# The first attention unit's scores and softmax in two halves, with its loads as first part, mask, second part

## The chip, the cores and the metric

One core of one Trainium2 chip runs the kernel. The metric is device microseconds (us) of one execution; lower is better.

## The reference

The kernel computes three stages one after the other: a local attention with a few global tokens, and two feed-forward layers.

```python
# attention: B, H, Sl, D = 4, 8, 512, 64, 32 global tokens, window 32
out_g = np.matmul(sm(s_g), v_all)                    # global queries see all keys
mask = np.abs(pos[:, None] - pos[None, :]) <= window # local queries see the window
s_l = np.concatenate([s_lg, np.where(mask, s_ll, -1e9)], axis=-1)
out_l = np.matmul(sm(s_l), np.concatenate([v_g, v_l], axis=2))
# first layer, d_ff = 1536
x = (silu(x @ w_gate) * (x @ w_val)) @ w_out
# second layer, d_ff = 2048
h = x @ w_in
out = (np.maximum(h, 0) + alpha * np.minimum(h, 0)) @ w_out
```

## The kernel before, in words

The attention works in units. A local unit (class Local) is one batch and one pair of heads: 16 blocks of 32 queries (NB is 16), each against a stretch of 128 gathered keys. `mm` makes the scores of the unit into two PSUM banks, one per head; `soft(h)` does the softmax of one head in four pieces of 128 rows by 128 keys: on DVE an addition of the mask `lm` with a row minimum (the scores are negated), on ACT an exponential with a row sum. `t(h)` transposes the four pieces of a head on PE and copies them from PSUM to the tile `pt`; the copy goes to ACT or to DVE by `evac`, in the share that `cp0` gives while the head of the program runs. `pv` multiplies with the values on PE and scales by the reciprocal row sums on DVE into the tile `o`, of which there is one buffer. `to` transposes `o` on PE; for batch 0 ACT writes the high part of it into `xa` and DVE the low part. Each float32 feed-forward product is made of three products of such parts.

The program starts with the four local units of batch 0, here called u0 to u3. Their loads are first in SP's queue: the keys and queries `qk` of u0 in two parts, the mask, then `qk` and the values `v` of the other units and the first weights. Weights of the first layer come as 64-bit floats and are converted by ACT and DVE (`raw`, `dbl`, `y`, `yp` in the profile) into a high and a low half `w`. While they land, `heat` issues 98 small matmuls on PE. Then the first layer visits batch after batch (`g`, `v`, `acc` in the profile, line 273), with the attention of the next batch between its matmuls; from about 405 us on a part runs without recording (lines 1245 to 1456).

The order of the work until then is not that of the code. Every operation is recorded by a Planner, in atoms (the operations of one engine inside one `with nc.atom()` stay together). `order` plays the atoms through a list schedule with fixed costs, takes at each step, of those that are ready within LOOK, the one that is due first, and `flush` issues them. So every recorded instruction has line 273, and tiles have to tell them apart. A change in the first atoms can alter the order of all that is planned after them.

The prediction's steps speak of `mm` and `soft` of Local (lines 449 to 487), of `evac` with `cp0`, of `pv` and `to`, and of the list `steps` at line 1062, which gives the order in which the head is recorded.

Of the kernel before, what the change touches and what calls it, by code (L numbers as in the profile page):

```python
# [19 lines left out]
B, H, S, G, D = 4, 8, 512, 32, 64  # L20
# [7 lines left out]
NB = S // 32  # L28
NPOS = 26
WIN = 32 * NPOS  # L30
# [7 lines left out]
    lo0=0.0, lo1=0.0, lo2=0.0, lo3=0.0, hi0=0.0, hi1=0.25, hi2=0.25, hi3=0.5,  # L38
    wl0=2, wl1=2, wd=2, tsim=False,
    hq0=0.0, hq1=0.0, hq2=0.0, hq3=0.0, pr_s=0, pr_pv=0, pr_conv=0, pr_hilo=0, pr_st=0, pr_ld=0, pr_h=0,  # L40
    pr_xp=0, pr_acc=0, pr_lda=0, wage=3, w2n=2, w2max=200, cp0=0.5, cp1=0.0,
)


def pos(i):

    return 3 * (i // 2) + i % 2
# [275 lines left out]
def kernel(  # L323
# [11 lines left out]
    nc = Planner(tc)  # L335
# [49 lines left out]
    lm = attc.tile([128, 4, 128], BF16, name="lm")  # L385
# [6 lines left out]
    def att_bank():  # L392
        t = att_tags["list"][att_tags["i"] % len(att_tags["list"])]
        att_tags["i"] += 1
        return bank(t)
# [4 lines left out]
    def heat(n, cols):  # L400

        t = bank("g")
        with nc.atom():
            for _ in range(n):
                nc.tensor.matmul(
                    out=t[0:cols, 0:cols], lhsT=zero[:, 0:cols], rhs=zero[:, 0:cols], start=True, stop=True
                )
# [37 lines left out]
    class Local(Unit):  # L445
        def __init__(self, pair):
            self.pair = pair

        def mm(self):
            x = self.pair.qk  # L450
            self.s = [att_bank(), att_bank()]
            with nc.atom():
                for i in range(NB):
                    t, c = divmod(i, 4)
                    for h in (1, 0):
                        rows = slice(D * h, D * h + D)
                        nc.tensor.matmul(
                            out=self.s[h][32 * c:32 * c + 32, 128 * t:128 * t + 128],
                            lhsT=x[rows, WIN + 32 * i:WIN + 32 * i + 32],
                            rhs=x[rows, 32 * pos(i):32 * pos(i) + 128],  # L460
                            start=True,
                            stop=True,
                        )
            self.e = attp.tile([128, 2, 4, 128], F32, tag="e", name="e")
            self.sm = attp.tile([128, 16], F32, tag="sm", name="sm")[:, 0:8]
            self.mx = attp.tile([128, 16], F32, tag="mx", name="mx")

        def soft(self, h):
            with nc.atom():
                for t in range(4):  # L470
                    j = 2 * t + h
                    nc.vector.tensor_tensor_reduce(
                        out=self.e[:, h, t],
                        in0=self.s[h][:, 128 * t:128 * t + 128],
                        in1=lm[:, t],
                        scale=-0.125,
                        scalar=3e38,
                        op0=ALU.add,
                        op1=ALU.min,
                        accum_out=self.mx[:, j:j + 1],  # L480
                    )
                for t in range(4):
                    j = 2 * t + h
                    nc.scalar.activation(
                        out=self.e[:, h, t], in_=self.e[:, h, t], func=ACTF.Exp, scale=-1.0, bias=self.mx[:, j:j + 1],
                        accum_out=self.sm[:, j:j + 1],
                    )
# [219 lines left out]
    def wload(now=False):  # L707
        if wq and not wq[0][3]:
            keys, src, pool, _, age = wq[0]
            if st["w"] < age + P["wage"] and not now:  # L710
                return False
            wq.popleft()
            at = pool.next("w")
            t = wtile(pool)
            if callable(src):
                src(t, at)
                return True
            with pr("ld"):
                nc.sync.dma_start(out=t.bitcast(F32), in_=src)
            put(keys, t)  # L720
            return True
        if wq and len(wloaded) < (ND if st["k"] < mark[2] - 4 else 2):
            keys, src, pool, _, _ = wq.popleft()
            raw = dbl_tile()
            with pr("ld"):
                nc.sync.dma_start(out=raw.rearrange("p (i c) -> p i c", i=2), in_=src)
            wloaded.append([keys, raw, pool, st["w"]])
            return True
        return False
# [50 lines left out]
    def wpump():  # L780
        ready = list(wsplit)
        wsplit.clear()
        wlow()
        while wloaded and wloaded[0][3] <= st["w"] - (P["wl0"] if st["k"] < mark[4] else P["wl1"]):
            e = wloaded.popleft()
            dbl = e[1]
            e[1] = raw = raw_tile()
            convert(dbl, raw)
            wsplit.append(e)
        for keys, raw, pool, _ in ready:  # L790
            raw = raw.rearrange("p (i c) -> p i c", i=2)
            t = wtile(pool)
            z = "0" if st["k"] < mark[1] else "1" if st["k"] < mark[2] else "2"
            with pr("hilo"):
                if frac("hi" + z):
                    nc.vector.tensor_copy(t[:, :, 0], raw)
                else:
                    nc.scalar.activation(out=t[:, :, 0], in_=raw, func=ACTF.Copy)
            wlo.append((keys, raw, t, st["w"], z))
        if not P["wd"]:  # L800
            wlow()
        st["w"] += 1
# [237 lines left out]

    if True:
        p0 = pairs[0]
        p0[0].load_qk(0)
        heat(HEAT, 128)
        heat(P["TINY"], 32)
        with nc.atom():
            p0[0].load_qk(1)
            nc.sync.dma_start(out=lm, in_=lmask)
        p0[1].load_qk()
        make_identity(nc.nc, ident)  # L1050
        p0[2].load_qk()
# [1 line left out]
        for f, p in zip((0, 1, 2, 3, 0, 4, 5, 2, 4), ("gv", "gv", "gv", "gv", "o", "gv", "gv", "o", "o")):  # L1053
# [6 lines left out]
        nc.sync.dma_start(out=gm[:, :, 0], in_=gmask)  # L1060
        u0, u1, u2, u3 = head
        steps = [
            [u0.mm, (u0.soft, 0), u1.mm, (u0.soft, 1)],
            [(u0.t, 0), (u1.soft, 0), (u0.t, 1), u2.mm, (u1.soft, 1)],
            [u0.pv, (u1.t, 0), (u2.soft, 0)],
            [u0.to, (u1.t, 1), u3.mm, (u2.soft, 1)],
# [6 lines left out]
        ]  # L1073
        for i, fs in enumerate(steps):
            for f in fs:
                f[0](f[1]) if isinstance(f, tuple) else f()
            if i >= 2:
                wload()
            wpump()
# [255 lines left out]
        for j in range(NF1 // 2):  # L1335
# [10 lines left out]
            h = hring[j % 2]  # L1346
# [239 lines left out]
```

## Time and profile before

| what | us |
|---|---|
| median of 3 runs | 885.64 (882.5 to 888.14) |
| the profiled execution | 882.67 |
| its span | 880.9 |
| PE busy | 865.6 (98%) |
| ACT busy | 527.1 (60%) |
| DVE busy | 690.1 (78%) |

The span runs from the first to the last instruction; the profiled execution is 1.77 us longer, for what lies around it. PE is TensorE's matmul, PEld its weight load, DVE VectorE, ACT ScalarE, SP the queue that issues the transfers. A row of the timeline gives start, duration, engine, line, operation, tiles written and read, and in brackets the idle time of the engine before it and what ended that; "issue" is a wait for which the profile shows no releaser.

### The profile page before, as it was taken

Reading aid. Unit: us, or ns where it says so; the run is one execution under the profiler, and the core shown is the slowest. Engines: PE = TensorE matmul, PEld = TensorE weight load, DVE = VectorE, ACT = ScalarE, POOL = GpSimd, SP = SyncE. Lnnn points to the kernel's source line nnn. Section 1 sums busy time; section 2 is a strip of 40 time slices with the busy share of each in tenths; the row PEclk is TensorE's granted clock in tenths of the full one; section 3 lists DMA queues with packets and bytes.
Section 4 is the critical chain, followed back from the end, with each engine's and each line's share of the span. In section 5 each row is a group of like instructions: output and inputs, shape, how many; then the busy total and the mean of one; then the engine's idle time right before and its main releaser. Section 6 shows DMA issues by size and latency. Waiting matters only on the chain.

```text
span 880.9 us, 17473 instructions
## 1 busy us (share of the span) xinstructions
PE 865.6 (98%) x6946; PEld 750.5 (85%) x6946; DVE 690.1 (78%) x1441; ACT 527.1 (60%) x1051; POOL 0.7 (0%) x6
## 2 busy tenths in 40 slices
PE   7899999999999999999999999999999999999997
PEld 6677778888788777888999999988999988999996
DVE  4897999989877857597766697777896777967776
ACT  6899999878586877654333346343645434553442
POOL 0000000000000000000000000000000000000000
PEclk8999999999999999999999999999999999999999
DMA  9899899899969799985566576364474645585631
GB/s 350 327 399 405 346 363 379 321 366 384 414 240 353 282 334 337 371 296 183 169 246 227 186 273 239 144 244 186 193 279 178 257 168 214 218 301 214 273 144 61
DMA packets 41666, 239.31 MB, mean 272 GB/s; under 512 B 4848, under 2 KB 5488, under 8 KB 19312
## 3 DMA queue, kind: packets, MB, share of 16 engines
q1 hardware_dynamic: 41584, 238.19, 71.6%
q8 instruction: 55, 0.90, 0.4%
q14 instruction: 27, 0.22, 0.1%
HBM read 183.38 MB, written 54.79 MB: 270 GB/s over the span
## 4 chain that ended last, share of the span: by engine, by line
PE 89%; DMA 5%; ACT 2%; DVE 2%; issue 1%; SPq 0%; ACTq 0%; DVEq 0%
PE ps_acc L1456 21%; PE acc L273 11%; PE g L273 10%; PE ps_g L1245 9%; PE ps_v L1245 9%; PE v L273 9%; PE ps_a L1245 8%; PE a L273 6%; PE ps_acc L1302 3%; PE ps_a L1302 2%; DMA dbl<-in_w_dram 1%; DMA qk<-in_qk_dram 1%; DMA w2so<-dbl 1%; DMA w2sx<-dbl 1%; DMA yp<-in_w_dram 1%
## 5 line engine op out<-in xcount | busy, mean ns | idle before, releaser
L1456 PE MATMUL ps_acc<-w,hring 128*128 128x512 f32 x816 | 194.2, 391 | 0.0
L1456 PEld LDWEIGHTS ps_acc<-w,hring 128*128 128x128 f32 x816 | 152.0, 188 | 30.1 <-ACT hring L1425 0.3
L273 PE MATMUL g<-xa,w 128*128 128x512 f32 x432 | 107.7, 397 | 1.0 <-ACT sg L273 0.4
L273 PE MATMUL v<-xa,w 128*128 128x512 f32 x432 | 107.0, 396 | 0.0
L273 PE MATMUL acc<-h,w 128*128 128x512 f32 x432 | 106.1, 394 | 0.0
L1420 ACT ACTIVATE r<-c 128x384 f32<-128x384 f32 (+1 forms) x96 | 47.9, 498 | 93.2 <-DVE c L1253 93.2
L1461 DVE TENSOR_TENSOR oacc<-ps_acc,oacc 128x512 f32<-128x512 f32 x119 | 81.9, 691 | 21.9 <-PE ps_acc L1456 20.7
L273 PEld LDWEIGHTS g<-xa,w 128*128 128x128 f32 x432 | 79.0, 188 | 20.8 <-ACT sg L273 1.5
L273 PEld LDWEIGHTS acc<-h,w 128*128 128x128 f32 x432 | 79.8, 188 | 18.6 <-issue 1.8
L273 PEld LDWEIGHTS v<-xa,w 128*128 128x128 f32 x432 | 79.3, 188 | 18.4 <-issue 1.4
L1425 ACT ACTIVATE hring<-g 128x384 fp32r<-128x384 f32 (+1 forms) x96 | 48.6, 506 | 55.8 <-DVE g L1422 55.5
L1426 DVE TENSOR_TENSOR hring<-g,hring 128x384 fp32r<-128x384 f32 (+1 forms) x96 | 51.1, 532 | 18.9 <-ACT hring L1425 16.1
L1422 DVE SCALAR_TENSOR_TENSOR g<-g,nal,r 128x384 f32<-128x384 f32 (+1 forms) x96 | 56.8, 591 | 10.6 <-ACT g L1421 10.0
L273 ACT ACTIVATE e<-e,mx 128x128 f32<-128x128 f32 (+1 forms) x136 | 57.2, 423 | 10.6 <-DVE mx L273 10.3
L273 ACT ACT_TABLE_LOAD x46 | 59.0, 1283 | 5.6 <-PE g L273 4.1
L1421 ACT ACTIVATE g<-c 128x384 f32<-128x384 f32 (+1 forms) x96 | 47.9, 499 | 13.7 <-DVE hring L1426 13.7
L1245 PE MATMUL ps_g<-xa,w 128*128 128x320 f32 (+1 forms) x288 | 53.4, 319 | 0.2
L1245 PE MATMUL ps_v<-xa,w 128*128 128x320 f32 (+1 forms) x288 | 53.2, 319 | 0.1
L1245 PE MATMUL ps_a<-w 128*128 128x384 f32 (+1 forms) x288 | 51.4, 326 | 0.0
L1245 PEld LDWEIGHTS ps_g<-xa,w 128*128 128x128 f32 x288 | 47.1, 188 | 1.9 <-ACT p L1261 0.4
L1245 PEld LDWEIGHTS ps_v<-xa,w 128*128 128x128 f32 x288 | 46.9, 188 | 1.6 <-DVE u L1269 0.4
L1245 PEld LDWEIGHTS ps_a<-w 128*128 128x128 f32 x288 | 47.9, 188 | 0.1
(209 smaller groups left out, 1403.1 us busy)
## 6 DMA issues: line engine op xcount, KB each, us to landing
dbl<-in_w_dram SPq DMA_DIRECT2D x28, 1024.0 KB, 7.7
w<-w2so SPq DMA_DIRECT2D x24, 1024.0 KB, 5.3
w<-w2sx SPq DMA_DIRECT2D x24, 1024.0 KB, 4.8
w<-w2ss SPq DMA_DIRECT2D x24, 1024.0 KB, 6.8
v<-in_v_dram SPq DMA_DIRECT2D x15, 1024.0 KB, 10.8
qk<-in_qk_dram SPq DMA_DIRECT2D x14, 688.0 KB, 8.7
w2sx<-dbl SPq DMA_DIRECT2D x8, 1024.0 KB, 5.9
w2so<-dbl SPq DMA_DIRECT2D x8, 1024.0 KB, 9.2
```

The source lines that it names most:

```text
L273: last[o.eng] = getattr(getattr(self.nc, o.eng), o.op)(*o.args, **o.kw)
L1245: nc.tensor.matmul(out=o[:, 0:n], lhsT=left(name, a, k), rhs=x[name][:, b, k, 0:n], start=(i == 0), stop=(i == 5),)
L1302: mm = nc.tensor.matmul(out=o, lhsT=a, rhs=x, start=(first and e == 0 and not second), stop=((j, f, e) == (NF1 // 2 - 1, 0, 2) and i not i ...
L1420: nc.scalar.activation(out=rr, in_=u, func=ACTF.Relu)
L1421: nc.scalar.activation(out=g, in_=u, func=ACTF.Relu, scale=-1.0)
L1422: nc.vector.scalar_tensor_tensor(out=g, in0=g, scalar=nal[:, i:i + 1], in1=rr, op0=ALU.mult, op1=ALU.add)
L1425: nc.scalar.activation(out=hi, in_=g, func=ACTF.Copy)
L1426: nc.vector.tensor_tensor(out=lo, in0=g, in1=hi, op=ALU.subtract)
L1456: nc.tensor.matmul(out=o, lhsT=a, rhs=x, start=(i == 0), stop=(i == 5))
L1461: nc.vector.tensor_tensor(out=oacc[tb], in0=o, in1=oacc[tb], op=ALU.add)
```

## The change

Three things are edited. `mm` can put its score matmuls into several atoms, and `soft` can take some of the four pieces; u0 uses both with two halves. The two parts of u0's `qk` and the mask are one atom, recorded in the order first part, mask, second part, ahead of `heat`. And `cp0` goes from 0.5 to 0.75: six instead of four of the eight copies of `pt` in the head are made by DVE.

```diff
-    pr_xp=0, pr_acc=0, pr_lda=0, wage=3, w2n=2, w2max=200, cp0=0.5, cp1=0.0,
+    pr_xp=0, pr_acc=0, pr_lda=0, wage=3, w2n=2, w2max=200, cp0=0.75, cp1=0.0,
...
-        def mm(self):
+        def mm(self, halves=1):
             x = self.pair.qk
             self.s = [att_bank(), att_bank()]
-            with nc.atom():
-                for i in range(NB):
...
+            for k in range(halves):
+                with nc.atom():
+                    for i in range(NB // halves * k, NB // halves * (k + 1)):
...
-        def soft(self, h):
+        def soft(self, h, ts=range(4)):
             with nc.atom():
-                for t in range(4):
+                for t in ts:
...
         p0 = pairs[0]
-        p0[0].load_qk(0)
+        with nc.atom():
+            p0[0].load_qk(0)
+            nc.sync.dma_start(out=lm, in_=lmask)
+            p0[0].load_qk(1)
         heat(HEAT, 128)
         heat(P["TINY"], 32)
-        with nc.atom():
-            p0[0].load_qk(1)
-            nc.sync.dma_start(out=lm, in_=lmask)
...
-            [u0.mm, (u0.soft, 0), u1.mm, (u0.soft, 1)],
+            [(u0.mm, 2), (u0.soft, 1, (0, 1)), (u0.soft, 0, (0, 1)), (u0.soft, 0, (2, 3)), u1.mm, (u0.soft, 1, (2, 3))],
```

In SP's queue before, the two transfers of the second part came first, then the mask, then the two of the first part; now the first part's two are first, the mask is third as before, and the second part's two follow. No other transfer moves until the 27th. The planner's order of the rest moves with the change. On PE, at the end of the transposes of u0 (`e_115` into `acc_125` and `acc_126`), the product of u0 with its values (`v_108` and `pt_123` into `a_113`) and the scores of u2 (`qk_102` into `v_129` and `g_103`) stand now as follows.

```order
 L273 MATMUL acc_125<-ident,e_115 128x128 x4
 L273 MATMUL acc_126<-ident,e_115 128x128 x4
+L273 MATMUL a_113<-v_108,pt_123 32x64 x32
 L273 MATMUL v_129<-qk_102 32x128
 L273 MATMUL g_103<-qk_102 32x128
```

The product of u0 with its values has gone from behind the 32 score matmuls of u2 to ahead of them (the trace shows each of these as two).

Further on PE, up to u3's product with its values (`yp_93` and `pt_124` into `g_103`), the transposes of u3's softmax (`e_116`) and of the results `o_130` of u1 (into `a_113`) and of u2 (into `acc_125`) change places.

```order
 L273 MATMUL g_103<-v_109,pt_124 32x64 x32
-L273 MATMUL acc_126<-ident,e_116 128x128 x4
 L273 MATMUL a_114<-qk_100 32x256 x2
 L273 MATMUL a_114<-qk_101 32x256 x2
+L273 MATMUL acc_122<-ident,e_116 128x128 x4
 L273 MATMUL a_113<-ident,o_130 128x128 x4
-L273 MATMUL acc_122<-ident,e_116 128x128 x4
 L273 MATMUL acc_121<-v_110,pt_123 32x64 x32
+L273 MATMUL acc_126<-ident,e_116 128x128 x4
+L273 MATMUL acc_125<-ident,o_130 128x128 x4
 L273 MATMUL g_103<-yp_93,pt_124 32x64 x32
-L273 MATMUL acc_125<-ident,o_130 128x128 x4
```

The transposes of u2's result now stand ahead of u3's product with its values instead of behind it.

On ACT, behind the first feed-forward blocks, the Silu of the second block (`sg_148`), the conversion of the next weights (`y_139`, `yp_95`) and two copies of transposes (`pt_123`) stand as follows.

```order
 L273 ACTIVATE w_135<-raw_132 128x2x512
+L273 ACTIVATE sg_148<-g_103 128x512
 L273 ACTIVATE y_139<-yp_95 128x1024
 L273 ACTIVATE yp_95<-yp_95 128x1024
 L273 ACTIVATE pt_123<-a_113 128x512
 L273 ACTIVATE pt_123<-a_114 128x256
-L273 ACTIVATE sg_148<-g_103 128x512
```

The Silu has moved ahead of the conversion and the copies.

## Rows read from the trace of the kernel before

**Rows 1.** The page, busy time of each engine and its share

```profile
PE 865.6 (98%) x6946; PEld 750.5 (85%) x6946; DVE 690.1 (78%) x1441; ACT 527.1 (60%) x1051; POOL 0.7 (0%) x6
```

**Rows 2.** Windows, 60 to 100 us: busy time per engine, clock, DMA share, GB/s

```profile
60.00:100.00 40.00, 40.00 (x433) 31.53 (x432) 33.50 (x78) 39.74 (x75) 0.00 (x0) 1.00 0.98 390
```

**Rows 3.** PE's waits from 45 to 400 us, longest total first: total, times, longest

```profile
PE a L273 <- ACT pt L273: 0.7, 1, 0.7
```

**Rows 4.** The chain that ended last: start, us, what

```profile
4.03 8.99 DMA qk<-in_qk_dram
...
50.12 2.95 PE g L273 x12
...
154.89 2.72 PE g L273 x12
```

**Rows 5.** Transfers to 30 us: KB each, median us from issue to landing

```profile
qk<-in_qk_dram SPq DMA_DIRECT2D x1, 224.0 KB, 4.1
...
lm<-in_lmask_dram SPq DMA_DIRECT2D x1, 128.0 KB, 3.4
```

**Rows 6.** Timeline of SP's queue, its first issues

```profile
0.74 0.88 SPq L273 DMA_DIRECT2D qk<-in_qk_dram  x2
1.66 0.43 SPq L273 DMA_DIRECT2D lm<-in_lmask_dram  x1
2.13 1.38 SPq L273 DMA_DIRECT2D qk<-in_qk_dram  x3
```

**Rows 7.** Timeline of PE, 6 to 50 us

```profile
6.71 1.15 PE L273 MATMUL a<-qk 64*32 64x128 f32 x64 [2.18 <-DMA qk<-in_qk_dram]
8.87 1.96 PE L273 MATMUL acc<-qk 64*32 64x128 f32 x64 [1.01 <-DMA qk<-in_qk_dram]
...
14.89 0.97 PE L273 MATMUL a<-v,pt 128*32 128x64 f32 x51
16.04 0.42 PE L273 MATMUL a<-v,pt 128*32 128x64 f32 x13 [0.18 <-issue]
...
22.24 0.66 PE L273 MATMUL g<-v,pt 128*32 128x64 f32 x33 [1.07 <-issue]
...
26.72 0.39 PE L273 MATMUL g<-yp,pt 128*32 128x64 f32 x10
28.94 1.71 PE L273 MATMUL g<-yp,pt 128*32 128x64 f32 x54 [1.84 <-issue]
30.59 1.12 PE L273 MATMUL acc<-ident,o 128*128 128x128 f32 x4
...
35.96 1.43 PE L273 MATMUL g<-xa,w 128*128 128x512 f32 x5 [0.31 <-DVE xa L273]
...
48.97 1.16 PE L273 MATMUL a<-qk 64*32 64x128 f32 x64 [0.72 <-ACT pt L273]
```

**Rows 8.** The page, the queue of instruction fetches: packets, MB, share

```profile
q8 instruction: 55, 0.90, 0.4%
```

**Rows 9.** Timeline of DVE, 7 to 32 us

```profile
7.92 0.29 DVE L273 CUSTOM_DVE_ANT_0 e<-a,lm 128x128 f32<-128x128 f32 x1 [6.98 <-PE a L273]
...
12.95 0.64 DVE L273 COPY pt<-acc 128x512 f32<-128x512 f32 x1
15.08 0.29 DVE L273 CUSTOM_DVE_ANT_0 e<-v,lm 128x128 f32<-128x128 f32 x1 [1.49 <-PE g L273]
...
25.66 1.23 DVE L273 SCALAR_TENSOR_TENSOR dbl<-dbl 128x1024 int32<-128x1024 int32 x1
...
31.74 0.69 DVE L273 TENSOR_TENSOR o<-g,rc 128x512 f32<-128x512 f32 x1 [2.33 <-PE acc L273]
```

**Rows 10.** Groups of 0 to 15 us: busy us, mean ns, idle before

```profile
L273 ACT ACTIVATE e<-e,mx 128x128 f32<-128x128 f32 x15 | 5.8, 388 | 6.2 <-DVE mx L273 6.2
```

**Rows 11.** Timeline of ACT, 17 to 28 us

```profile
17.09 0.60 ACT L273 ACTIVATE pt<-a 128x512 f32<-128x512 f32 x1
...
27.59 1.16 ACT L273 ACTIVATE y<-yp 128x1024 f32<-128x1024 f32 x1 [1.01 <-DMA yp<-in_w_dram]
```

More of the change, by code (lines that the diff above doesn't have):

```diff
@@ L447, in __init__ @@
             self.pair = pair
-        def mm(self):
+        def mm(self, halves=1):
             x = self.pair.qk
             self.s = [att_bank(), att_bank()]
-            with nc.atom():
-                for i in range(NB):
[L454 to L463, printed above, removed]
+            for k in range(halves):
+                with nc.atom():
+                    for i in range(NB // halves * k, NB // halves * (k + 1)):
+                        t, c = divmod(i, 4)
+                        for h in (1, 0):
+                            rows = slice(D * h, D * h + D)
+                            nc.tensor.matmul(
+                                out=self.s[h][32 * c:32 * c + 32, 128 * t:128 * t + 128],
+                                lhsT=x[rows, WIN + 32 * i:WIN + 32 * i + 32],
+                                rhs=x[rows, 32 * pos(i):32 * pos(i) + 128],
+                                start=True,
+                                stop=True,
+                            )
             self.e = attp.tile([128, 2, 4, 128], F32, tag="e", name="e")
@@ L481, in soft @@
                     )
-                for t in range(4):
+                for t in ts:
                     j = 2 * t + h
@@ L1075 @@
             for f in fs:
-                f[0](f[1]) if isinstance(f, tuple) else f()
+                f[0](*f[1:]) if isinstance(f, tuple) else f()
             if i >= 2:
```

## The prediction

> **What bounds the kernel now.** I read the page's busy times first: PE is busy 98% of the span, and no other engine comes near it [rows 1]. The chain of waits agrees; from 50 us on its rows are nearly all blocks of 12 matmuls that follow each other. So what is left to win lies in the few places where PE waits. From 45 to 400 us the waits list has 0.7 us at its top, from one single wait [rows 3]. The rest of PE's idle time lies in the first 45 us, and I read those on the timelines of PE, DVE, ACT and SP.
>
> What the reader is to see there: PE makes u0's scores at 6.71, u1's at 8.87, and both times it waited for keys and queries to land [rows 7]. u2's keys were issued at 4.03 and needed 8.99 us, to 13.02 [rows 4]. Then PE stops three times inside a product with the values, with nothing to wait for: 0.18 us at 16.04, 1.07 at 22.24, 1.84 at 28.94 [rows 7]. I counted PE's records between these stops: 51 or 13 of the first product, then 128 matmuls with 128 weight loads to each next stop. That is 256 instructions a time. The page shows 55 packets of instructions with 0.90 MB, 16 KB each [rows 8]; 256 instructions of 64 bytes (an estimate from these two counts) are one packet. So I read the stops as waits for the next 16 KB of program, which come 6.2 us (16.04 to 22.24) and 6.7 us (22.24 to 28.94) after one another. The head is paced by keys landing until 13 us, and by PE's program from 16 to 29.
>
> **The change part by part.** *The halves.* Before, the first part's transfers were issued fourth and fifth. Now they are first, at 0.74, and the mask stays third, at 1.66 [rows 6]. The 224 KB transfer took 4.1 us in the fourth place, so first it should be there by 0.74 + 4.1 = 4.8 at the latest; the mask needs 3.4 us, to 1.66 + 3.4 = 5.1 [rows 5, 6]. PE is free from 4.53 (6.71 less its 2.18 idle). So DVE can start u0's softmax at about 5.2 instead of 7.92 [rows 9], 2.7 us earlier. The second half's keys land when the last ones did, near 6.6, which gives its scores by 7.3. ACT's exponentials take 388 ns each and waited 6.2 us for DVE [rows 10]; all eight can now be done by 9.5 or so, not 11.3. But what needs them on PE is u0's transposes, and these stand behind u1's scores, which start at 8.87 for their keys and end at 10.8 [rows 7], as before. The third and following transfers land as before, since the sum of bytes ahead of them is the same. So I cost this part at 0: the landing of u1's and u2's keys hides it. If that cover were gone, it would be worth the 2.7 us at the most; below nothing it can hardly be, since no transfer is added.
>
> *Two copies from ACT to DVE.* Each takes 0.60 us on ACT [rows 11] and 0.64 on DVE [rows 9]. ACT gets about 1.0 us of room (pipelined, two take about 0.5 each), DVE, which waits between its softmaxes, loses 1.2. Alone 0; it counts in the next item.
>
> *u0's product ahead of u2's scores.* It needs both copies of the transposes; DVE's is done at 12.95 + 0.64 = 13.6 [rows 9]. Before, PE filled 13.06 to 14.9 with u2's scores. The product takes between 64 x 0.97/51 = 1.2 us and 64 x 1.71/54 = 2.0, the two speeds that this form has in the trace [rows 7], so u2's scores begin between 14.9 and 15.7. They take 1.15 to 1.96 [rows 7], so DVE takes up u2 between 16.1 and 17.7, where it was 15.08 [rows 9]: 1.0 to 2.6 us late. I take 1.9, the slow product and the fast scores. Queued behind on ACT are the exponentials of u2 and u3 and the first weights' conversion. ACT gains back the 1.0 of the copies, and had 1.01 us idle before the weights that land at 27.5 [rows 11], so 0.9 us of delay is covered there. PE's product of u3 before was ready at 26.72 and stopped until 28.94, about 2 us after its 10 matmuls. In the new order u3's last copy on DVE stands behind one more conversion step of 1.23 us [rows 9]: 0.9 + 1.2 = 2.1 late, so about 28.7, when the program packet is due at 28.94. I take 0, with only 0.2 us to spare; it costs up to 1.9 us without this cover, and below zero there is nothing to gain.
>
> *u2's result ahead of u3's product.* Before, DVE waited 2.33 us until 31.74 to write u3's result into `o`, because PE's transposes of u2's result (30.59, 1.12 us) read the only buffer and stood behind the stopped product [rows 7, 9]. Now they are done before the stop. The stop then falls 6 matmuls into u3's product, 58 are left, 58 x 1.71/54 = 1.84 us, to 30.8. DVE goes on at 30.8 instead of 31.74: -0.9 us, and all behind it on DVE (the low halves of the first weights and of `xa`) is as much earlier. PE's first block ended at 35.96 + 1.43 = 37.4 after two waits for DVE [rows 7], so it should end near 36.5. Bounds: -1.2, when the short waits inside that block go as well, and +0.6, when the program packets come later by what u2's scores are late (16.6 for 16.04 at the same record).
>
> On these packets a page can be held against the trace. The Trainium skill, Runtime: NRT & Kernel Launch, Instruction fetch mechanics, says that the engine's next 16 KB are fetched while it executes the current ones, and that the cost of crossing is mostly hidden. The size agrees with the trace, the hiding does not: 1.84 us at 28.94 [rows 7]. By its first half, a page begun 0.55 us later brings the next ones as much later, this item would be -0.4 and my sum 0.5 us less of a gain; by fixed arrivals it is -0.9.
>
> *The Silu ahead of two copies.* PE waited 0.72 us at 48.97 for a copy by ACT to free a bank for the next scores [rows 7]. In the new order the Silu is done before the weights' conversion, so the next feed-forward block can go ahead of these scores, about 3 us that cover the copy. -0.7, at the least 0.
>
> *The order after that.* The number of times PE goes from small attention matmuls to blocks of 12 goes from 64 to 65 by the order of instructions; a block behind such a change takes 2.95 us where one behind another block takes 2.72 [rows 4], so +0.2. What the new order costs in waits the trace can't tell. PE has hardly a wait left to lose between 50 and 400 us, so this is 0 or more; the nearest large one is the 1.84 of the head. I take +0.4, near the low end, because a similar plan had only one wait of size.
>
> The sum: -0.9 - 0.7 + 0.2 + 0.4 = -1.0 us. On the profiled execution 882.67 - 1.0 = 881.7 (its span 879.9). That execution was 3.0 us under the median of the runs, so on the median it is 885.64 - 1.0 = 884.6.
>
> **The rivals.** *Given back later (885.6).* From 60 to 100 us ACT is busy 39.74 of 40 us, and the transfers run at 0.98 of what they can [rows 2]. If the weights' conversion on ACT sets the pace there, an earlier start only makes PE wait there, and the change is worth 0. Against it: PE was busy all 40 us.
>
> A rule of the Trainium skill speaks for this rival: Trainium Kernel Development and Optimization, Performance Expectations, has it that matmul busy time says little and weight loads tell more. Here PEld was busy 31.53 of those 40 us [rows 2], which by that rule leaves room in PE and makes ACT the bound.
>
> *The early product delays all (887.4).* The place is u0's product ahead of u2's scores. If it makes u3's product start later than 28.94, the packet no longer covers it, the 1.9 us go into the end, and the gain at u2's result is lost: +1.9 - 0.7 + 0.2 + 0.4 = +1.8. For it: 0.2 us of cover. Against it: ACT's idle time ahead of 27.59.
>
> *The early softmax comes through (882.8).* If the exponentials and not the keys pace the head, the whole 2.7 us stay in place of the 0.9, with the other terms as above: -2.7 - 0.7 + 0.2 + 0.4 = -2.8. Against it: the chain of waits goes through u2's keys, not through u0's softmax.
>
> **How the numbers follow.** The forecast has 0.45, given back later 0.25, the delay 0.2, the early softmax 0.1. A measurement of this kernel can tell about 1%, 8.9 us, from no change; all cases lie within it. For faster or slower by more the new order after 50 us would have to move nine us: 0.03 for faster, where nothing in the trace has that much to give, 0.05 for slower, 0.92 within. The range: below, the early softmax less 2 us, about a third of the runs' spread of 5.6, by which a new median can lie off: 882.8 - 2.0 = 880.8; above, the delay with the upper bound of the waits, 887.4 + (1.84 - 0.4) = 888.8.
>
> **What would show it.** Right: DVE's first softmax row near 5.2, u1's scores still at 8.87, u2's softmax on DVE at 16 to 17, the 256-instruction stops still there with the third ending near 29, u3's result on DVE near 30.8, no wait at 48.97. The forecast is wrong if u3's product starts after 29, if PE's waits from 50 to 400 us add to more than 2 us, or if u1's scores come before 8.87.

## The result and the profile after

The changed kernel takes 890.47 us (median, 887.25 to 892.59), the kernel before 883.38 beside it: ratio 1.0067, 95% interval 1.005 to 1.0085. So it is 0.7% slower, some 6 us by the ratio (the two medians lie 7.1 apart), where I had forecast 1.0 us less and a range that ended at 888.8. It lies within the 1% that had 0.92.

The profiled execution took 891.28 us with a span of 889.5, 8.6 more than before. Part of that is chance: the execution of before that was profiled took 882.67, near the lowest of its runs (881.58 to 888.14). First the page's busy times, which answer to [rows 1].

```profile
PE 868.6 (98%) x6946; PEld 750.4 (84%) x6946; DVE 691.0 (78%) x1443; ACT 523.2 (59%) x1047; POOL 0.7 (0%) x6
```

PE is busy 3.0 us longer with the same number of instructions, and idle 889.5 - 868.6 = 20.9 us instead of 15.3: 5.6 of idle time and 3.0 of busy time make the 8.6. Where the idle time lies is read from the windows. The columns are: stretch, its length, PE's busy time, granted clock, DMA share, GB/s; first the kernel after, then two stretches of before.

```profile
0.00:60.00 60.00, 48.87 (x875) 0.91 0.87 332
60.00:100.00 40.00, 39.80 (x477) 1.00 1.01 412
100.00:200.00 100.00, 98.78 (x1067) 1.00 0.88 343
200.00:300.00 100.00, 99.00 (x946) 1.00 0.83 329
300.00:410.00 110.00, 109.38 (x970) 1.00 0.84 321
410.00:420.00 10.00, 8.81 (x50) 1.00 0.48 166
```

```profile
100.00:200.00 100.00, 100.00 (x1133) 1.00 0.93 355
200.00:300.00 100.00, 100.00 (x952) 1.00 0.85 330
```

Before, PE had no idle time from 60 to 300 us, 0.36 from 300 to 410 and 0.20 to 420. After, the rows from 60 us on add to 0.20 + 1.22 + 1.00 + 0.62 + 1.19 = 4.23 us: 3.7 of the 5.6 come from here. The first 60 us, where the edit is, have 0.9 more, and the transfer of the last output adds 0.9. The waits list of PE from 45 to 420 us (total, times, longest) gives the idle time its names; [rows 3] is its counterpart, with one wait of 0.7 at the top.

```profile
PE a L273 <- issue: 1.2, 1, 1.2
PE ps_g L1246 <- DVE u L1254: 1.2, 1, 1.2
PE v L273 <- DVE t L273: 0.9, 1, 0.9
PE acc L273 <- DVE h L273: 0.6, 1, 0.6
PE g L273 <- ACT sg L273: 0.6, 1, 0.6
PE acc L273 <- ACT h L273: 0.4, 1, 0.4
PE acc L273 <- DVE w L273: 0.2, 1, 0.2
```

Seven small waits, six for five different operands and one for the program, and no large one: `t`, `h`, `sg`, `w` and `u` all come late somewhere. I read that as another order and not as a new bottleneck; the list alone doesn't show it, and the experiments below test it. Their places are seen in PE's timeline; the first rows are the head, and answer to [rows 7].

```profile
4.47 0.89 PE L273 MATMUL a<-qk 64*32 64x128 f32 x32
6.47 0.67 PE L273 MATMUL a<-qk 64*32 64x128 f32 x32 [1.12 <-DVE mx L273]
7.86 1.86 PE L273 MATMUL acc<-qk 64*32 64x128 f32 x64 [0.72 <-DMA qk<-in_qk_dram]
...
12.47 0.99 PE L273 MATMUL a<-v,pt 128*32 128x64 f32 x56 [0.49 <-DVE pt L273]
...
17.74 0.27 PE L273 MATMUL g<-qk 64*32 64x128 f32 x1 [3.30 <-issue]
...
30.39 0.32 PE L273 MATMUL g<-yp,pt 128*32 128x64 f32 x8
31.68 1.20 PE L273 MATMUL g<-yp,pt 128*32 128x64 f32 x56 [0.97 <-DVE pt L273]
...
35.89 3.03 PE L273 MATMUL g<-xa,w 128*128 128x512 f32 x12
...
54.84 3.04 PE L273 MATMUL v<-xa,w 128*128 128x512 f32 x12 [0.91 <-DVE t L273]
...
109.00 0.41 PE L273 MATMUL a<-qk 64*32 64x128 f32 x4 [1.22 <-issue]
...
415.26 1.14 PE L1246 MATMUL ps_g<-xa,w 128*128 128x320 f32 x6 [1.19 <-DVE u L1254]
```

The halves do what they say: u0's scores come in two pieces, and u0's product stands ahead of u2's scores. But the program stops PE for 3.30 us inside u2's scores, where the longest of the three stops before was 1.84. By a count in PE's timeline it is the stop of before, at the same place of the program: behind the 349th matmul, which PE reached at 15.86 before and at 14.44 now. What differs is when PE went on, 16.04 before and 17.74 now. The first block of twelve ends at 35.89 + 3.03 = 38.9, where it ended at 37.4 and I expected 36.5. On DVE's timeline the same is seen at u0's first softmax, at u2's, and at u3's result; these answer to [rows 9].

```profile
5.48 0.29 DVE L273 CUSTOM_DVE_ANT_0 e<-a,lm 128x128 f32<-128x128 f32 x1 [4.55 <-PE a L273]
...
18.25 0.29 DVE L273 CUSTOM_DVE_ANT_0 e<-v,lm 128x128 f32<-128x128 f32 x1 [4.04 <-PE g L273]
...
33.27 0.68 DVE L273 TENSOR_TENSOR o<-g,rc 128x512 f32<-128x512 f32 x1
```

The softmax starts 2.4 us earlier (7.92 before); 13 us on, u2's is 3.2 us later (15.08), and u3's result 1.5 later (31.74).

These differences of the head are not yet the edit's. `x1_old_head_new_rest`, `x5_new_order_at_the_end_only`, `x6_new_order_in_the_middle_only`, `x9_tensor_order_old_rest_new` and `x10_tensor_order_new_rest_old` (below) have the head of the kernel before, atom for atom. In their traces u1's scores start between 8.56 and 10.80 (8.87 before), and the third stop ends between 27.98 and 30.37 (28.94 before). So one and the same head moves by 2 us from one execution to another.

### The profile page after: what moved, and what is told of

It is laid out like the page before. It is cut to its first block, busy times and chain, and to the rows that moved or that the text cites. A ratio compares the mean times of both kernels' runs of the same rounds, so it can differ in the third digit from the quotient of the medians.

```text
span 889.5 us, 17441 instructions
## 1 busy us (share of the span) xinstructions
PE 868.6 (98%) x6946; PEld 750.4 (84%) x6946; DVE 691.0 (78%) x1443; ACT 523.2 (59%) x1047; POOL 0.7 (0%) x6
## 4 chain that ended last, share of the span: by engine, by line
PE 75%; DVE 10%; DMA 7%; ACT 5%; issue 2%; SPq 0%; ACTq 0%; DVEq 0%
PE ps_acc L1457 21%; PE ps_g L1246 10%; PE ps_v L1246 9%; PE ps_a L1246 8%; PE acc L273 6%; PE v L273 6%; PE g L273 6%; PE a L273 4%; DMA w2ss<-raw 3%; PE ps_acc L1303 3%; DVE raw L273 2%; PE ps_a L1303 2%; DVE dbl L273 2%; DVE y L273 2%; ACT e L273 1%
## 5 line engine op out<-in xcount | busy, mean ns | idle before, releaser
L273 ACT ACTIVATE e<-e,mx 128x128 f32<-128x128 f32 (+1 forms) x136 | 57.2, 423 | 18.6 <-DVE mx L273 17.7
L1427 DVE TENSOR_TENSOR hring<-g,hring 128x384 fp32r<-128x384 f32 (+1 forms) x96 | 51.1, 532 | 18.9 <-ACT hring L1426 16.1
```

The costliest lines, as they stand in the source:

```text
L273: last[o.eng] = getattr(getattr(self.nc, o.eng), o.op)(*o.args, **o.kw)
L1427: nc.vector.tensor_tensor(out=lo, in0=g, in1=hi, op=ALU.subtract)
```

## The experiments

The planner's order is a list of atoms. In most of these kernels the list is written out, so that the planner cannot answer an edit with another order. The edit is then always this one, with `PLAN` told in words:

```diff
-        for i in self.order():
+        for i in PLAN:
```

An atom of the head is any up to the 131st planned one of the kernel before, the 134th of the changed one (the change makes three more). Behind this cut both plans hold the same atoms, in two orders: 19 of PE's atoms, 200 of DVE's, 93 of ACT's and 51 of SP's leave their place (counted as the fewest that must move to turn one order into the other).

**Head and rest apart.** `x1_old_head_new_rest` is the kernel before, with its own head and the changed kernel's order behind it.

> The kernel before, issued in its own order for the four units of the head, and in the changed kernel's order from there on (the two orders have the same set of work done at that point). Theory A, the loss is made in the head and passed on (the changed kernel's first feed-forward block ended 1.5 us late, its second weights landed 3.4 us late): 883 to 884.5, as the kernel before. Theory B, the order after the head makes most of the loss (waits of 1.2 us at 109, 1.0 at 230, 1.2 at 415 that the kernel before does not have): 887 to 889.5.

Measured: 889.95 us, ratio 1.0065 (1.0046 to 1.0085). Nothing of the edit is in this kernel, and it has the whole loss. Its waits of PE from 45 to 420 us show the changed kernel's pattern again, in an execution of its own:

```profile
PE ps_g L1245 <- DVE u L1253: 1.2, 1, 1.2
PE a L273 <- issue: 0.8, 1, 0.8
PE g L273 <- ACT sg L273: 0.8, 1, 0.8
PE acc L273 <- ACT h L273: 0.8, 1, 0.8
PE v L273 <- DVE t L273: 0.6, 1, 0.6
PE acc L273 <- DVE h L273: 0.6, 1, 0.6
...
```

The loss lies behind the head here. PE starts its third block into `v` no later than the kernel before does, whose row is shown first:

```profile
53.48 2.99 PE L273 MATMUL v<-xa,w 128*128 128x512 f32 x12
```

```profile
53.34 3.04 PE L273 MATMUL v<-xa,w 128*128 128x512 f32 x12 [0.64 <-DVE t L273]
```

The spans of these two executions are 880.9 and 887.6, and nearly all of the 6.7 us comes behind that row (six small transposes, 0.6 us, have moved behind it as well).

`x2_new_head_old_rest` is the converse: the changed kernel with its head, and the order of before from there on.

> The changed kernel, its own order for the head, and from there on the order of the kernel before. Theory A: 888 to 890.5, as the changed kernel. Theory B: 884 to 885.5, the late head alone. Both theories can hold in part, then both hybrids lie between; if the loss needs both at once, both lie near 883.

Measured: 884.76 us, ratio 1.0011 (0.9995 to 1.0026). The whole edit of the head is worth nothing that can be told from 0, and no gain. In its trace u1's keys came 3 us later than in the changed kernel, and the stop for the program was 0.23 us and not 3.30, at the same 349th matmul:

```profile
11.02 1.96 PE L273 MATMUL acc<-qk 64*32 64x128 f32 x64 [3.87 <-DMA qk<-in_qk_dram]
...
18.00 0.27 PE L273 MATMUL g<-qk 64*32 64x128 f32 x1 [0.23 <-issue]
```

So the long stop is not made by this head alone. The two halves of the difference, 0.65% and 0.11%, add to the 0.67% within their intervals.

`x3_halves_and_loads_alone` keeps only the halves and the order of the transfers; `cp0` is 0.5 again, and the order is that of before from the 35th atom on.

> The changed kernel with cp0 back at 0.5: the loads and u0's halves as changed, all the rest in the order of the kernel before. Theory A in the form that u0's product ahead of u2's scores does the harm: 882.5 to 884, nothing lost, nothing won, since u2's keys land when they did. Theory A in the form that the earlier loads alone move PE's instruction packet (3.3 us of stop at 14.4 in the changed kernel, 0.18 at 16.0 before): the stop is there again with 2 to 3 us, and 885 to 887. Theory B: 882.5 to 884.

Measured: 884.83 us, ratio 0.9998 (0.998 to 1.0015). The part that I costed at 0 is 0. In its trace PE has done u0's transposes early and then waits for u2's keys, which land about when they did (13.06 before); the program's stop behind them is 0.96 us:

```profile
13.18 0.29 PE L273 MATMUL v<-qk 64*32 64x128 f32 x1 [1.20 <-DMA qk<-in_qk_dram]
```

This run also warns against reading an order from one list of waits. Its order behind the head is that of before, and still PE waits 4.5 us from 45 to 420 us in its profiled execution, which took 886.61 and was the longest of its twelve:

```profile
PE a L273 <- ACT pt L273: 3.1, 3, 1.8
...
```

`x4_product_back` is the changed kernel with u0's product and the scaling of its result put back behind u2's scores and softmax.

> The changed kernel in its own order, only u0's product with its values (and its scaling on DVE) put back behind u2's scores and softmax. Theory A with the early product as the cause: u2's softmax on DVE starts near 15 instead of 18.25, the first feed-forward block ends near 37.4 instead of 38.9, and the time falls by 2 us or more, to 885 to 888. If the stop for instructions stays at its record and PE gets there anyway, the 128 matmuls end the same and the time stays at 889 to 891. Theory B: 889 to 890.5.

Measured: 889.29 us, ratio 1.0059 (1.0041 to 1.0077), against 1.0067 with the early product. The intervals lie over each other. By itself this leaves room for a part of the loss; but `x1_old_head_new_rest` has the whole loss without the early product, and `x2_new_head_old_rest` has the product without the loss.

**Which part of the rest.** At the 899th planned atom (near 300 us) both orders again have the same atoms behind them. `x5_new_order_at_the_end_only` has the order of before up to there and the new one from there.

> The kernel before, its own order up to its 899th planned piece (about 285 us), then the changed kernel's order to the end. The earlier run with the changed order from the 131st piece on lost 5.7 us. If its loss sits at its visible waits, 0.82 us for sg at 388 and 1.19 us for u at 414 are in this part and 2.5 us in the part ahead of it: +1.5 to +2 here, about 886. Rival, the loss is made ahead of the 899th piece alone and the wait at 414 is only what was already late: 0, about 884.2. Rival, the end makes most of it: +4 or more.

Measured: 886.37 us, ratio 1.0015 (0.9996 to 1.0034), or 1.3 us, which the interval does not quite tell from 0, with the end's own wait in place:

```profile
...
PE ps_g L1245 <- DVE u L1253: 1.2, 1, 1.2
...
```

`x6_new_order_in_the_middle_only` has the new order only between the 131st and the 899th.

> The kernel before with the changed kernel's order only between its 131st and 899th planned pieces (about 50 to 285 us), its own order ahead and behind. By the visible waits of the earlier run (0.64 at 53, 0.32 at 71, 0.84 for the program at 107, 0.78 and 0.58 for h at 228) and some 1 us of shorter runs of one kind of matmul: +3.5 to +4, about 888, and with the run of the end alone it adds up to the 5.7. Rival, the two parts do not add, because work put off in the middle is paid at the end: under +2.

Measured: 891.08 us, ratio 1.0071 (1.0044 to 1.0097). I had expected less, and the profile shows why the run doesn't isolate the middle: at the seam, where the order of before takes over, PE waits once for 4.2 us.

```profile
PE a L273 <- ACT pt L273: 4.2, 1, 4.2
...
```

Before has no such wait. The twelve matmuls behind it took 4.60 us, with a granted clock of 0.55 from 301.5 to 303.5; twelve of that form take 3.0 elsewhere. So the seam alone costs some 5.8 us in this execution. As I read it, ACT reaches the seam late in the new order, and the old order behind it has PE ask for a copy that the new one would have left for later. So work put off in the middle is paid at its end, and how the loss is shared between the two parts stays open. The end alone is the smaller part, as expected.

**Which engine.** `x9_tensor_order_old_rest_new` is the kernel before in which, behind its head, PE keeps its order while DVE, ACT and SP take theirs from the changed kernel; `x10_tensor_order_new_rest_old` is the converse. PE's two orders differ in little: in most places one group of twelve feed-forward matmuls stands one or two atoms earlier.

> The kernel before with its own head; behind it TensorE keeps its old order, the vector, scalar and sync engines take theirs from the changed kernel. Theory, the loss is made by the other engines' order, which hands TensorE's operands over late: +4 to +6, 888 to 890. Rival, the loss is made by TensorE's own order (16 groups of twelve matmuls stand one place earlier, so that they meet operands that are not ready and attention's pieces come later): 0 to +1.5. Third, the two orders were made for each other and each alone is worse than both: over +6.

> The converse: TensorE's order from the changed kernel, the other three engines as before. Theory, the other engines' order makes the loss: 0 to +2. Rival, TensorE's own order makes it: +4 to +6. Third, made for each other: over +3 here and over +6 in the converse.

Measured: 896.16 us, ratio 1.0133 (1.0111 to 1.0155), and 904.15 us, ratio 1.0235 (1.021 to 1.026). Neither engine's order makes the loss by itself; both mixtures are far worse than either kernel, which is the third case that I had set down. The waits of PE from 45 to 420 us, first with PE's order old, then with it new:

```profile
PE a L273 <- DVE mx L273: 3.4, 2, 1.7
PE a L273 <- ACT pt L273: 2.9, 4, 1.3
PE a L273 <- DVE o L273: 2.1, 2, 1.4
PE g L273 <- ACT sg L273: 1.9, 2, 1.7
...
```

```profile
PE acc L273 <- DVE h L273: 4.3, 4, 1.9
PE g L273 <- ACT sg L273: 3.7, 3, 1.9
PE v L273 <- DVE t L273: 2.6, 1, 2.6
PE acc L273 <- ACT h L273: 2.5, 3, 1.3
...
```

The reader can see which way each fails. With the old order PE goes to attention's pieces first, and waits for what attention needs (`mx`, `pt`, `o`); with the new one it goes to the feed-forward blocks first, and waits for what these need (`h`, `sg`, `t`). In the kernel before and in the changed one, as I read it, each order meets the operands of its own plan.

**Is any other order slower?** Two kernels without any part of the change, in which one number of the planner is moved a little.

```diff
-    SLACK=60.0, LOOK=0.1, SWITCH=4.0, MARGIN=0.5, HEAT=8, TINY=90, ND=3, NR=3, LAG=6,
+    SLACK=60.0, LOOK=0.12, SWITCH=4.0, MARGIN=0.5, HEAT=8, TINY=90, ND=3, NR=3, LAG=6,
```

> The kernel before without any part of the change; only the planner's LOOK is 0.12 in place of 0.1, which gives yet another order (194 of the vector engine's pieces behind the head leave their place, as many as in the change). Theory, the old order is one that its numbers were fitted to and any other order of this planner costs some us: +2 to +6, 886 to 890. Rival, the changed kernel drew a poor order by its own waits and other orders are about as good as the old one: within 1 us of the kernel before.

Measured: 888.75 us, ratio 1.0043 (1.0026 to 1.006). The second has `MARGIN=0.55` in the same line and `LOOK` as before.

> The kernel before without any part of the change; only the planner's MARGIN is 0.55 in place of 0.5 (133 of the vector engine's pieces leave their place, 6 of TensorE's). Theory, any other order costs some us: +1.5 to +6. Rival, other orders are about as good: within 1 us. Together with the run of LOOK 0.12: if one is slow and one is not, an order's time is drawn anew each time and the change's 5.7 us say little of the change itself.

Measured: 893.81 us, ratio 1.0096 (1.0061 to 1.0131). And the changed kernel with its third edit undone:

```diff
-    pr_xp=0, pr_acc=0, pr_lda=0, wage=3, w2n=2, w2max=200, cp0=0.75, cp1=0.0,
+    pr_xp=0, pr_acc=0, pr_lda=0, wage=3, w2n=2, w2max=200, cp0=0.5, cp1=0.0,
```

> The changed kernel with cp0 back at 0.5: the halves and the order of the first transfers stay, and the planner draws its own order, which behind the head is a third one (138 of the vector engine's pieces stand elsewhere than before, 189 elsewhere than in the changed kernel; it is also what the kernel before gets from cp0 = 0.75 alone). The same halves and transfers with the old order took 884.8. Theory, any order but the old one costs some us: +2 to +8. Rival, this third order happens to be as good as the old one: within 1 us.

Measured: 894.08 us, ratio 1.0103 (1.0079 to 1.0127). This is the run to set beside `x3_halves_and_loads_alone`: the same halves, transfers and copies, once with the order of before (0.9998) and once with the order that the planner makes of them (1.0103). The order alone is 1%, the edit nothing. So all four other orders of this planner that were run, the changed kernel's among them, are slower than that of the kernel before, by 0.4 to 1.0%, whether an edit came with them or not. The number of atoms that leave their place does not say how much: 194 of DVE's cost 0.43% (`x7_before_look_0p12`), 133 cost 0.96% (`x8_before_margin_0p55`). Why the order of before is the fastest of the five no run shows.

**The best of both.** `x12_new_head_product_back_old_rest` is the changed kernel's head with u0's product put back, and the order of before behind it.

> The changed kernel's first 134 planned pieces, with u0's product put back behind u2's scores and softmax, and from there on the order of the kernel before. The same without the product put back took 884.8 (ratio 1.001), and putting the product back in the changed kernel gave 1.2 us. Theory, what the edit does in the head is worth nothing to the span because the blocks behind it wait for weights and operands of their own: 0, 883.5 to 885. Rival, with the old order behind it a better head comes through: -1 or more, 882.5, and this would beat both kernels.

Measured: 885.38 us, ratio 1.0011 (0.9993 to 1.0029). No gain; no kernel here beats the one before. The head did get better in the trace: the first block of twelve ends at 33.91 + 2.57 = 36.5, which is what I had forecast for it, instead of 37.4. But PE's only wait from 45 to 420 us is the 0.72 us of [rows 7], now 1.82 long:

```profile
33.91 2.57 PE L273 MATMUL g<-xa,w 128*128 128x512 f32 x10 [0.76 <-DVE w L273]
...
49.24 1.16 PE L273 MATMUL a<-qk 64*32 64x128 f32 x64 [1.82 <-ACT pt L273]
```

PE goes on at 49.24, where it went on at 48.97 before. ACT's copy stands behind the conversion of the weights `yp`, and that began at 46.29, when their transfer had landed (45.97 before). `x3_halves_and_loads_alone` is alike: its first block is done at 36.35, and PE goes on at 49.02.

## Why the prediction was wrong

**The failing step is the order after that.** I wrote "What the new order costs in waits the trace can't tell", bounded it by 0 and 1.84, and took "+0.4, near the low end, because a similar plan had only one wait of size". By `x1_old_head_new_rest` the order behind the head costs 0.65%, 5.7 us, three times the upper end. (That run also holds the Silu's move and the transitions, so my forecast for it was -0.7 + 0.2 + 0.4 = -0.1.) Several things were wrong with the bound. It was one wait of the head, while an order in which hundreds of atoms move can make a wait wherever an operand now comes late; the changed kernel has seven from 50 us on. The plan before was no typical plan from which a neighbour differs by a little: four neighbours were all slower by 0.4 to 1.0%. Of the "similar plan" no run here shows anything. That PE "has hardly a wait left to lose" came from one execution, a short one; `x3_halves_and_loads_alone`, with the same order behind its head, had 4.5 us of waits in a longer one. I read it as a floor under the loss; I now take it rather as a sign that an arrangement was there to be lost.

**The halves, 0: right**, by `x3_halves_and_loads_alone`, and for the reason given: u2's keys hide them there. DVE began at 5.48 in the changed kernel, for my 5.2. That the following transfers land as before can't be tested to 1 us: u1's scores came at 7.86 in the changed kernel instead of 8.87, and at 11.02 in `x2_new_head_old_rest` with the same transfers. The chain of waits after has the keys that released them at 3.08 + 4.73 = 7.81:

```profile
3.08 4.73 DMA qk<-in_qk_dram
```

In that execution PE did not wait for u2's keys; what stood behind the gain was the program's stop.

**The early product, 0, with cover by the packet due at 28.94: right as a cost, but the cover could not be read from one trace.** `x2_new_head_old_rest` and `x12_new_head_product_back_old_rest` differ in this product alone, and both lie at +0.11%. The times that I gave were missed: in the changed kernel u3's product started at 30.39, past the 29 that I had named as the sign, u2's softmax at 18.25 instead of 16.1 to 17.7, and the last 56 matmuls of u3's product then waited 0.97 us for DVE's copy, so in this execution the packet covered nothing. In `x2_new_head_old_rest` it did: there PE stopped 1.00 us for the program inside u3's product, until 30.72. I had reckoned with packets that come at their old times or 0.55 us later; in heads without any edit the third one came between 27.98 and 30.37, and 0.2 us of cover is far less than that. (My count of 128 matmuls from stop to stop holds to the second; to the third the trace has 127.)

**u2's result ahead of u3's product, -0.9: won in the head, then lost.** The wait of 2.33 us in front of u3's result is gone, as the step says. In the changed kernel that result is written at 33.27, not at 30.8, because the product ahead of it is late. In `x12_new_head_product_back_old_rest` it is written at 30.85 and the first block ends at 36.5, both as forecast; then PE waits until 49.24 for ACT's copy, and the run gains nothing. In that trace this is the rival "given back later", which I had at 0.25, with the mechanism that it names, at 49 us instead of behind 60: the weights' conversion on ACT sets the pace, and an earlier start only makes PE wait there.

**The Silu ahead of the copies, -0.7: the wait went, the gain is not seen.** The wait at 48.97 is gone, and 0.91 for `t` at 54.84 is new. The 0.59 for `sg` at 43.70 is not of this move: `x2_new_head_old_rest`, with the Silu in its old place, has 0.74 there. `x1_old_head_new_rest` starts the block behind `t` at 53.34, 53.48 before, so next to nothing is lost up to there. None of the rivals held the loss; the one that was slower, at 887.4, put it at the early product, and `x1_old_head_new_rest` and `x2_new_head_old_rest` show that it isn't there.

**What stays open.** The transitions (+0.2) were not measured alone. The 3.0 us by which PE is busy longer I can't assign: u3's 64 scores took 1.96 us behind the long stop, at a granted clock of 0.50, where the same form took 1.16 before (+0.8), but u3's product took 1.5 instead of 2.1 (-0.6); blocks of `acc<-h` add 1.0 in their group and score matmuls of `a<-qk` 1.3. Which atom's move makes which wait behind 60 us was not tried one by one, and by `x9_tensor_order_old_rest_new` and `x10_tensor_order_new_rest_old` it may have no answer for one engine alone.

## What to carry to other kernels

Where a planner turns the program into an order, an edit is two changes, the edit and a new draw of the order, and the draw can be the larger: here 0 to 0.1% and 0.65%. Pin the old order and try the edit by itself, and move a number of the planner that has nothing to do with the edit, to see how far apart neighbouring orders lie, before a difference is put down to the edit. And when PE waits nowhere, bound the cost of a new order by the times of several such orders, not by one wait of the old, and not by the number of atoms that move. Read the length of a single wait from several executions: here the same head moved by 2 us between them.

## What the runs showed of the hardware

The stops for the program keep their place in the program and not their length: 55 packets and 0.90 MB both times [rows 8], but 0.18, 1.07 and 1.84 us before in the head, and one of 3.30 after. By a count in PE's timelines they come behind the 349th matmul and, within one matmul, every 128 further on; with the head of before, atom for atom, the stop at the 349th is 0.15 us in `x10_tensor_order_new_rest_old` and 1.22 in `x1_old_head_new_rest`. In the new order there is also one far from the head: 1.22 us at 109 in the changed kernel, 0.8 in `x1_old_head_new_rest`, 0.9 in `x6_new_order_in_the_middle_only` and 1.9 in `x4_product_back`, the four kernels that have the new order in the middle on all engines, and none there before. The transfers ran at a share of 1.01 from 60 to 100 us in the changed kernel, 0.98 before [rows 2]; that this is the cause is not shown.

A wait of PE can cost more than its own length. In `x8_before_margin_0p55` PE waited 2.05 us for `h`; the granted clock behind it was 0.50 of full, the lower of its two levels, and eleven matmuls took 3.95 us that took 2.79 in `x1_old_head_new_rest`. First the timeline of `x8_before_margin_0p55` and its window (columns as above), then the timeline of `x1_old_head_new_rest`:

```profile
228.33 0.68 PE L273 MATMUL acc<-h,w 128*128 128x512 f32 x1 [2.05 <-ACT h L273]
229.40 3.95 PE L273 MATMUL acc<-h,w 128*128 128x512 f32 x11 [0.39 <-DVE h L273]
```

```profile
229.00:231.00 2.00, 1.61 (x5) 0.50 1.04 430
```

```profile
229.03 2.79 PE L273 MATMUL acc<-h,w 128*128 128x512 f32 x11 [0.58 <-DVE h L273]
```

So the wait of 2.05 us cost about 1.2 more. It was alike behind the 4.22 us at the seam of `x6_new_order_in_the_middle_only` (clock 0.55, 1.6 more), and behind 2.66 us in `x7_before_look_0p12`, where 64 small matmuls took 1.94 us at a clock of 0.50 and 1.10 elsewhere. Behind the waits of 0.78 and 0.58 in `x1_old_head_new_rest`, of 1.22 at 109 in the changed kernel and of 1.91 at 107 in `x4_product_back` the matmuls ran at full speed. The length alone doesn't decide it: at one and the same place the 1.82 us of `x12_new_head_product_back_old_rest` had, one step behind it, a block of 4.62 us (clock 0.56 from 50.3 to 52.3), the 1.83 of `x3_halves_and_loads_alone` one of 3.00. I had priced every wait at its length.
